# Layer two of batch 4 in seven half-size products, with the squares and sums divided among three engines and all pieces in a new order

## The chip, the cores and the metric

The kernel runs on one core of a Trainium2 chip. The core has a matrix engine (TensorE, PE in the profile; its weight loads are PEld), VectorE (DVE), ScalarE (ACT), GpSimd (POOL) and SyncE (SP). Each has its own queue of instructions that it works through in order; semaphores order one engine behind another. Matrix products go to PSUM, from where VectorE or ScalarE fetch them into SBUF. DMAs are issued from the queues of SP, POOL and ACT. The metric is device time in microseconds. Before the change it is 224.83 us (median of three runs, 224.76 to 225.58).

## The reference

Batches B = 8, heads H = 8, tokens S = 512, states Ns = 32, D = 64, so a token of all heads has H*D = 512 elements. Attention goes both ways between the tokens x and the states, and the result passes through two layers with a squared relu between them:

```python
scores  = scale * np.matmul(x, state.transpose(0, 1, 3, 2))      # softmax over the states
xread   = np.matmul(a, state)
scores2 = scale * np.matmul(state, x.transpose(0, 1, 3, 2))      # softmax over the tokens
sread   = np.matmul(a2, x)
x = concatenate([xread, sread], axis=2).transpose(0, 2, 1, 3).reshape(B * (S + Ns), H * D)
h = x @ w_in                       # 512 -> 2048
r = np.maximum(h, 0.0)
g = s * (r * r) + b
return (g @ w_out).astype(np.float32)   # 2048 -> 512
```

## The kernel before

Layers and attention are worked batch by batch on 512 token rows; the 8 x 32 state rows ("sr") are gathered from all batches and pass through the layers at the end. The attention's second product is folded into the first layer: M = state times w_in is made per batch, so that layer one is the softmax weights A times M.

**Pieces.** Everything is cut into pieces, and the list ORDER names them one after the other. Each piece emits its instructions at once, so ORDER fixes the order in every engine's queue; nothing else schedules. A name holds the piece, the batch, its part, and at the end often the engine (A ScalarE, V VectorE, G GpSimd). Those of the prediction's steps:

- `x.b`, `xn.b`, `win.j`, `wout.q`: loads of x in two layouts, and of quarters of w_in and w_out, from GpSimd's queue. `castx`, `casts`: casts of batch 0's x and first states, which come as FP32 on SP's and ACT's queues.
- Attention of batch b: `xT` (transpose), `T` (scores, TensorE), `U` (transpose back), `mu` (maximum over the states), `D` (difference), `E1` (exponential), `z` (sum and reciprocal), `At` (times reciprocal), `A` (transpose). Batch 0 has these in halves. `keep` copies the scores from PSUM to SBUF. The other direction: `nm`, `nms`, `E2`, `a2`, `aps`, `a2T`, `V`, `srd`.
- `M.b.j` (TensorE) and `Mc.b.j` (copy out of PSUM): a quarter of M. T, M, aps, V and `turn` (transposing the states) use two PSUM tiles of two banks each; the next user of a tile waits for the reader of the last.
- `l.b.f`: one of 16 blocks of layer one, two matmuls of 512 columns on TensorE and a relu on ScalarE into a buffer r of four blocks (`lh`, half the tokens, for batch 0's first blocks, with buffers rh). `s.b.f.n.E`: the square of n blocks from f on, on engine E, into g (`sh` for the halves). `lsr`, `ssr`: the same for the state rows.
- `L.b.rr.q`: four of the 16 matmuls (512 columns) that make 128 rows of the output; four rr by four q make a batch. `out.b.rr` scales, adds the bias and stores. `cps`, `c`, `bias` make the bias from w_out.
- `idle.n`: n matmuls that compute nothing.

**Seven products.** For batches 5, 6, 7 and the state rows layer two isn't done in L pieces. The 512 x 2048 by 2048 x 512 product is taken as 2 x 2 blocks, and seven products of half size take the place of eight: `P.b.u` is one half (8 matmuls of 256 columns) of product u // 2; the half u % 2 takes the even or odd blocks up to, or from, block 8. They need sums of blocks of g (`S.b.1` to `S.b.4`, in halves, S1, S2 and S4 in place, S3 in a tile of its own) and of w_out (`wsum.T1` to `T4`). Products X, W and Y stand in PSUM; `ev.b.X1`, `Y`, `X2`, `W1`, `X3`, `W2`, `X4` add them up in the output tiles osx0 and osx1 on VectorE, and `put` stores. X is added to in PSUM between its evictions, so the next X product waits for the eviction. S2 overwrites what the first product reads, and S4 what the second reads, so they wait for these. The state rows have `S_sr`, `P_sr`, `ev_sr` alike.

In the code, `act_sum` (lines 555 to 564), `weight_sum` (522 to 535) and `sum_sr` (613 to 622) take half h of four of eight block pairs:

```python
A = lambda i, j: block(b, i, j)[:, 4 * h : 4 * h + 4]
```

The buffers r (three) and rh (four) are taken from the pool `rpool` under one tag each, in `layer1` (449 to 456) and `layer1_half` (473 to 482); the squares are `squared` (458 to 462).

Of the kernel before, what the change touches and what calls it, by code (L numbers as in the profile page):

```python
# [11 lines left out]
FP16 = mybir.dt.float16  # L12
# [66 lines left out]
def kernel(  # L79
# [14 lines left out]
    ALU = mybir.AluOpType  # L94
# [6 lines left out]
    P = 128  # L101
# [346 lines left out]

    def layer1(tag, f, terms, ntok):
        hps = ps_h.tile([P, ntok], FP32, name=f"hps_{tag}_{f}", tag="ph")  # L450
        for i, (lhsT, rhs) in enumerate(terms):
            nc.tensor.matmul(hps, lhsT, rhs, start=(i == 0), stop=(i == len(terms) - 1))  # L452
        q, i = f // 4, f % 4
        if (tag, q) not in R_t:
            R_t[tag, q] = rpool.tile([P, 4, ntok], FP16, name=f"r_{tag}_{q}", tag="r")
        nc.scalar.activation(R_t[tag, q][:, i], hps, AF.Relu)  # L456
# [16 lines left out]
    def layer1_half(b, f, p):  # L473
# [7 lines left out]
        r = R_t[b, f, p] = rpool.tile([P, 2, HALF], FP16, name=f"rh_{b}_{f}_{p}", tag="rh", bufs=4)  # L481
# [37 lines left out]

    fast_w = {}  # L520

    def weight_sum(name, h, e):
# [3 lines left out]
        w = w_out16[:, 8 * h : 8 * h + 8]  # L526
        B = [[w[:, k::2, HALF * n : HALF * n + HALF] for n in range(2)] for k in range(2)]
        T = {k: t[:, 4 * h : 4 * h + 4] for k, t in fast_w.items()}
# [26 lines left out]
    def act_sum(b, name, h, e):  # L555

        A = lambda i, j: block(b, i, j)[:, 4 * h : 4 * h + 4]
        out, x, y, op = {
            1: lambda: (A(1, 0), A(1, 0), A(1, 1), ALU.add),
            2: lambda: (A(0, 0), A(1, 0), A(0, 0), ALU.subtract),  # L560
            3: lambda: (fast(b, "S3")[:, 4 * h : 4 * h + 4], A(0, 0), A(1, 0), ALU.subtract),
            4: lambda: (A(0, 1), A(0, 1), A(0, 0), ALU.subtract),
        }[name]()
        e.tensor_tensor(out, x, y, op)  # L564
# [182 lines left out]
```

## Time and profile before

| | |
|---|---|
| median of three runs | 224.83 us |
| the profiled execution | 224.36 us, of which the span is 222.2 us |
| TensorE busy | 210.7 us, 95% of the span |
| VectorE, ScalarE, GpSimd busy | 183.6, 141.8, 43.4 us |
| granted TensorE clock | 1.0 |
| chain that ended last | TensorE 88%, DMA 4%, VectorE 3%, ScalarE 3% |

The span is from the first to the last recorded event; the profiled execution's time has 2.16 us around it. In the rows of groups of instructions the columns are line, engine, operation, what it writes and reads, shapes and count, then busy time in us, mean ns of one, and the idle time just before with its releaser. Rows of the timeline and of the chain begin with the start and the length in us. A matmul's mean (380 ns) holds its way through the array; rows of the chain give the spacing of successive ones. Rows of stretches give, after the length, busy time and count of PE, PEld, DVE, ACT and POOL, then the granted clock, the DMA share and GB/s. In the 40 slices a digit is the busy share in tenths of 5.55 us.

### The profile page before, as it was taken

The numbers are of one execution on the slowest core, as the hardware profiler recorded it, in microseconds if no ns is written. First come the engines' busy times: TensorE is split into PE (matmuls) and PEld (weight loads), VectorE is DVE, ScalarE is ACT, GpSimd is POOL, SyncE is SP. The second block draws the span as 40 slices with busy tenths as digits, with TensorE's granted clock in tenths as the row PEclk, the third lists the DMA queues.
The fourth block names the chain that finished last, engine by engine and source line by source line (L and its number), as shares of the span: only waits on it lengthen the run. The fifth ranks groups of instructions, "written<-read, shape, count | busy, mean of one in ns | idle before, by whom it ended". The sixth has DMA issues, their size and how long they took to land.

```text
span 222.2 us, 4473 instructions
## 1 busy us (share of the span) xinstructions
PE 210.7 (95%) x1816; PEld 115.8 (52%) x1816; DVE 183.6 (83%) x267; ACT 141.8 (64%) x243; POOL 43.4 (20%) x73
## 2 busy tenths in 40 slices
PE   6469999999999999999999999999999999999992
PEld 2234334444444443444454544457766778888881
DVE  1597998889769997989796799889999997966772
ACT  2475895776488869855787479485877858533400
POOL 8245504000273400046002160005200000000000
PEclk9999999999999999999999999999999999999999
DMA  6999993420557892048927397226903500440066
GB/s 158 227 207 206 205 193 58 101 72 20 100 112 117 112 174 50 16 100 120 192 47 133 96 128 124 49 45 101 141 2 65 127 0 3 94 99 0 3 134 149
DMA packets 23416, 22.67 MB, mean 102 GB/s; under 512 B 4196, under 2 KB 16996, under 8 KB 23396
## 3 DMA queue, kind: packets, MB, share of 16 engines
q0 software_dynamic: 16560, 12.26, 38.6%
q1 hardware_dynamic: 6160, 9.97, 18.2%
q8 instruction: 14, 0.23, 0.4%
q10 hardware_dynamic: 676, 0.16, 0.3%
q14 instruction: 6, 0.05, 0.1%
HBM read 25.72 MB, written 8.91 MB: 156 GB/s over the span
## 4 chain that ended last, share of the span: by engine, by line
PE 88%; DMA 4%; DVE 3%; ACT 3%; SPq 1%; issue 0%
PE ops L496 31%; PE hps L452 24%; PE opf_X L137 9%; PE opf_W L137 5%; PE mps L137 4%; DMA xf<-in_x_dram 4%; PE hps_sr L452 3%; PE opf_Y L137 2%; PE vps L137 2%; PE T_None L137 2%; PE aps L137 2%; PE ops_sr_X L137 2%; ACT M L152 1%; DVE xT L289 1%; PE ops_sr_W L137 1%; ACT rh L482 1%
## 5 line engine op out<-in xcount | busy, mean ns | idle before, releaser
L456 ACT ACTIVATE r<-hps 128x512 f16<-128x512 f32 x120 | 69.3, 610 | 29.8 <-PE hps L452 28.4
L496 PE MATMUL ops<-w_out,g 128*128 128x512 f16 x320 | 78.1, 379 | 1.3 <-DVE g L462 1.3
L452 PE MATMUL hps<-A,M 128*128 128x512 f16 x240 | 65.3, 380 | 0.5 <-DVE M L152 0.3
L496 PEld LDWEIGHTS <-g 128*128 128x128 f16 x320 | 30.3, 98 | 38.4 <-issue 2.8
L462 DVE TENSOR_TENSOR g<-r 128x1024 f16<-128x1024 f16 (+1 forms) x39 | 34.5, 897 | 8.1 <-ACT r L456 8.0
L452 PEld LDWEIGHTS <-M 128*128 128x128 f16 x240 | 21.9, 98 | 25.8 <-issue 4.7
L137 PEld LDWEIGHTS <-g 128*128 128x128 f16 x288 | 28.0, 98 | 6.4 <-issue 0.2
L152 ACT CAST M<-mps 128x1024 f16<-128x1024 f32 x28 | 28.0, 1013 | 1.8 <-PE mps L137 1.8
L192 POOL DMA_DIRECT2D xn<-in_x_dram x32 | 18.5, 588 | 29.2 <-PE vps L137 28.3
L506 DVE SCALAR_TENSOR_TENSOR osb<-ops,sb_bc,bias_bc 128x512 f32<-128x512 f32 x20 | 14.7, 734 | 1.0 <-PE ops L496 1.0
L180 POOL COPY ahead<-xT 1x2 f16<-1x2 f16 x5 | 1.8, 367 | 67.0 <-DVE xT L289 67.0
L456 ACT ACTIVATE r_sr<-hps_sr 128x256 f16<-128x256 f32 x16 | 6.2, 385 | 12.8 <-PE hps_sr L452 12.4
L564 DVE TENSOR_TENSOR g<-g 128x1024 f16<-128x1024 f16 x18 | 12.2, 685 | 2.0 <-PE opf_Y L137 1.9
L289 DVE STREAM_TRANSPOSE xT<-xh 128x1024 f32<-128x1024 f32 (+2 forms) x12 | 10.3, 871 | 3.2 <-ACT xh L152 3.2
L333 DVE TENSOR_REDUCE z<-E 128x32 f32<-128x1024 f16 (+1 forms) x9 | 9.9, 1095 | 3.7 <-ACT E L328 3.7
L137 PE MATMUL opf_X<-w_T,g 128*128 128x256 f16 x96 | 11.9, 273 | 0.0
L137 PE MATMUL mps<-w_in,stT 64*32 64x512 f16 x256 | 11.2, 383 | 0.2 <-ACT M L152 0.2
L318 DVE TENSOR_REDUCE mu<-U 128x32 f32<-128x1024 f32 (+1 forms) x9 | 9.9, 1097 | 0.2
L376 ACT ACTIVATE E<-T_None,nms 128x512 f16<-128x512 f32 x8 | 5.5, 691 | 6.9 <-DVE nms L372 4.4
L328 ACT ACTIVATE E<-Dm 128x1024 f16<-128x1024 f32 (+1 forms) x9 | 8.7, 963 | 1.8 <-DVE Dm L322 1.5
L322 DVE TENSOR_TENSOR Dm<-U,mu 128x1024 f32<-128x1024 f32 (+1 forms) x8 | 9.6, 1201 | 0.2
L314 DVE STREAM_TRANSPOSE U<-T_None 128x1024 f32<-128x1024 f32 x7 | 8.7, 1247 | 1.2 <-PE T_None L137 0.8
(94 smaller groups left out, 259.4 us busy)
## 6 DMA issues: line engine op xcount, KB each, us to landing
out_dram<-osb SPq DMA_DIRECT2D x32, 128.0 KB, 2.7
xn<-in_x_dram POOLq DMA_DIRECT2D x32, 128.0 KB, 5.7
xh<-in_x_dram POOLq DMA_DIRECT2D x14, 256.0 KB, 5.2
out_dram<-osx SPq DMA_DIRECT2D x24, 128.0 KB, 2.4
w_in<-in_moe_w_in_dram POOLq DMA_DIRECT2D x8, 256.0 KB, 10.6
w_out<-in_moe_w_out_dram POOLq DMA_DIRECT2D x4, 512.0 KB, 12.7
xf<-in_x_dram SPq DMA_DIRECT2D x4, 256.0 KB, 7.5
out_dram<-osb SPq DMA_DIRECT2D x4, 256.0 KB
```

What stands on the lines that cost most here:

```text
L137: return nc.tensor.matmul(out, lhsT, rhs, start=start, stop=stop, tile_position=tp, is_transpose=is_transpose, skip_group_check=skip,)
L152: (engine.copy if engine is nc.scalar else engine.tensor_copy)(out, in_)
L192: nc.gpsimd.dma_start(out=xn_t[b][32 * jh : 32 * jh + 32].rearrange("t h c d -> t h (c d)"), in_=x[b].rearrange("h (t jh c) d -> jh t h (c ...
L289: nc.vector.transpose(part(out, p, g), part(in_, p, g))
L318: nc.vector.tensor_reduce(part(mu, p), blk(part(at[b]["U"], p)), AX.X, ALU.max)
L333: nc.vector.tensor_reduce(part(z, p), blk(part(at[b]["E1"], p)), AX.X, ALU.add)
L452: nc.tensor.matmul(hps, lhsT, rhs, start=(i == 0), stop=(i == len(terms) - 1))
L456: nc.scalar.activation(R_t[tag, q][:, i], hps, AF.Relu)
L462: e.tensor_mul(g, r, r)
L496: nc.tensor.matmul(ops_t[tag, rr], G_t[tag][:, f, P * rr : P * rr + P], w_out_f(f), start=(f == 0), stop=(f == NKF - 1),)
L506: nc.vector.scalar_tensor_tensor(osb, ops_t.pop((tag, rr)), s_bc, bias_bc, ALU.mult, ALU.add)
L564: e.tensor_tensor(out, x, y, op)
```

## The change

- Batch 4's layer two goes from 16 L and 4 `out` pieces to 14 P, 7 evictions and 4 puts, with its sums S; the sums of w_out are made earlier accordingly.
- Squares, sums, casts of M, D and At are spread differently over ScalarE, VectorE and GpSimd. GpSimd, which had four half squares and one D, gets 9 squares, 5 half squares, 7 sums S, 4 sums of the state rows, 2 weight sums, 2 At and 3 D.
- A sum can be taken whole: `HALVES` has a third entry, h = 2, for all eight block pairs.
- r and rh are taken under one tag per buffer, in turn.
- The idle matmuls are 2, 5 and 9, all ahead of the first scores; they were 11, 6 and 4, the six and the four further on.
- All pieces stand in a new order, the loads too: after w_in's first two quarters it was wout.0, x.1, win.2, wout.1, win.3; it is x.1, win.2, wout.0, win.3, wout.1.

```diff
-    "win.0 win.1 wout.0 x.1 win.2 wout.1 win.3 wout.2 wout.3 idle.11 castx.1.0.V castx.0.0.A xT.0.0.0 "
+    "win.0 castx.0.0.V castx.1.0.A idle.2 idle.5 idle.9 casts.V xT.0.0.0 pair.0.4 xT.0.1.0 T.0.1.0 U.0.0 "
+    "sb mu.0.0 win.1 castx.1.1.A xT.0.1.1 x.1 D.0.V.0 E1.0.0 castx.0.1.V xT.0.0.1 turn.0.4.A z.0.0 "
+    "At.0.V.0 A.0.0 M.0.0.0 Mc.0.0.A keep.0.0 win.2 T.0.0.1 U.0.1 M.0.1.1 Mc.0.1.A mu.0.1 D.0.V.1 "
+    "keep.0.1 E1.0.1 xT.1.0 lh.0.2.0 M.1.0.0 Mc.1.0.A lh.0.0.0 xT.1.1 T.1.1 lh.0.6.0 wout.0 z.0.1 "
+    "At.0.V.1 A.0.1 lh.0.2.1 win.3 U.1 M.0.2.0 lh.0.0.1 Mc.0.2.V wout.1 sh.0.2.1.V keep.1 sh.0.0.0.G mu.1 "
+    "sh.0.2.0.G lh.0.4.0 wout.2 sh.0.4.0.G D.1.V L.0.0.0 l.0.11 M.1.1.0 Mc.1.1.A L.0.1.0 l.0.8 sh.0.6.0.V "
+    "l.0.9 M.0.3.0 Mc.0.3.V M.1.2.1 x.2 l.0.10 Mc.1.2.V wout.3 E1.1 z.1 lh.0.6.1 At.1.V s.0.8.2.A L.0.0.1 "
+    "l.0.13 L.0.1.1 l.0.14 cps.0 cps.1 cps.2 M.1.3.1 A.1 Mc.1.3.V l.0.12 s.0.12.2.V s.0.10.2.G l.0.15 "
+    "s.0.14.2.A L.0.1.2 l.1.4 l.1.7 L.0.0.2 l.1.1 l.1.2 sh.0.6.1.V st xT.2 x.3 pair.4.16 cps.3 L.0.0.3 "
+    "L.0.1.3 c bias lh.0.4.1 l.1.5 T.2.1 l.1.3 out.0.0 out.0.1 U.2 sh.0.0.1.G L.0.3.0 s.1.4.2.A l.1.6 "
...
+    "l.6.0 l.6.1 M.6.3.0 S.5.1.2.V Mc.6.3.A xn.7 xn.1 M.7.0.1 Mc.7.0.A l.6.7 ev.5.Y P.5.6 P.5.7 z.7 "
+    "S.5.2.2.V M.7.1.1 Mc.7.1.A E2.7.1 l.6.15 s.6.0.4.V l.6.14 nm.1 S.5.4.1.G P.5.4 P.5.5 ev.5.X2 ev.5.W1 "
+    "l.6.10 M.7.2.1 S.5.4.0.V E2.7.0 M.7.3.0 Mc.7.3.A At.7.V P.5.8 l.6.13 l.6.4 P.5.9 a2.7 l.6.11 "
...
+    "lsr.0 ssr.0.2.V P.7.8 P.7.9 ssr.2.2.V S_sr.3.0.V ev.7.X3 lsr.9 S.7.4.1.V lsr.8 P.7.10 P.7.11 "
+    "ssr.8.2.A ssr.10.2.V S_sr.3.1.G put.5.1.1 put.6.0.0 S_sr.1.2.V S_sr.2.2.G S_sr.4.0.G put.6.0.1 "
+    "put.6.1.0 put.6.1.1 ev.7.W2 P.7.12 put.7.0.0 put.7.0.1 P.7.13 ev.7.X4 P_sr.0 put.7.1.0 "
+    "ev_sr.0.0.X.0.0 P_sr.1 ev_sr.0.0.Y.1.1 P_sr.2 P_sr.3 put.7.1.1 S_sr.4.1.G ev_sr.0.1.X.0.0 P_sr.4 "
...
+    turns = {}
+
+    def in_turn(shape, name, tag, n):
+        k = turns[tag] = turns.get(tag, -1) + 1
+        return rpool.tile(shape, FP16, name=name, tag=f"{tag}{k % n}", bufs=1)
...
-            R_t[tag, q] = rpool.tile([P, 4, ntok], FP16, name=f"r_{tag}_{q}", tag="r")
+            R_t[tag, q] = in_turn([P, 4, ntok], f"r_{tag}_{q}", "r", 3)
...
+    HALVES = (slice(0, 4), slice(4, 8), slice(0, 8))
...
-        A = lambda i, j: block(b, i, j)[:, 4 * h : 4 * h + 4]
+        sl = HALVES[h]
+        A = lambda i, j: block(b, i, j)[:, sl]
```

More of the change, by code (lines that the diff above doesn't have):

```diff
@@ L480, in layer1_half @@
                 mm(hps[:, i, :], lhsT, part(A, p, g)[:, 0, :], start=(g == 0), stop=(g == NG - 1))
-        r = R_t[b, f, p] = rpool.tile([P, 2, HALF], FP16, name=f"rh_{b}_{f}_{p}", tag="rh", bufs=4)
+        r = R_t[b, f, p] = in_turn([P, 2, HALF], f"rh_{b}_{f}_{p}", "rh", 4)
         nc.scalar.activation(r, hps, AF.Relu)
@@ L525, in weight_sum @@
             fast_w[name] = konst.tile([P, NKF // 2, HALF], FP16, name=f"w_{name}", tag=f"w_{name}")
-        w = w_out16[:, 8 * h : 8 * h + 8]
-        B = [[w[:, k::2, HALF * n : HALF * n + HALF] for n in range(2)] for k in range(2)]
-        T = {k: t[:, 4 * h : 4 * h + 4] for k, t in fast_w.items()}
+        w = w_out16
+        B = [[w[:, k::2, HALF * n : HALF * n + HALF][:, HALVES[h]] for n in range(2)] for k in range(2)]
+        T = {k: t[:, HALVES[h]] for k, t in fast_w.items()}
         a, b = {
@@ L560, in act_sum @@
             2: lambda: (A(0, 0), A(1, 0), A(0, 0), ALU.subtract),
-            3: lambda: (fast(b, "S3")[:, 4 * h : 4 * h + 4], A(0, 0), A(1, 0), ALU.subtract),
+            3: lambda: (fast(b, "S3")[:, sl], A(0, 0), A(1, 0), ALU.subtract),
             4: lambda: (A(0, 1), A(0, 1), A(0, 0), ALU.subtract),
@@ L620, in sum_sr @@
         }[name]
-        out, x, y = (t[:, 4 * h : 4 * h + 4] for t in (S_sr(name), x, y))
+        out, x, y = (t[:, HALVES[h]] for t in (S_sr(name), x, y))
         e.tensor_tensor(out, x, y, op)
```

99 rows, old and new, of the table ORDER are left out of this document.

## The prediction

> **What bounds the kernel now.** I read the page's parts 1, 2 and 4 first, then TensorE's waits, then the timeline of the first 41 us.
>
> ```profile
> PE 210.7 (95%) x1816; PEld 115.8 (52%) x1816; DVE 183.6 (83%) x267; ACT 141.8 (64%) x243; POOL 43.4 (20%) x73
> PE   6469999999999999999999999999999999999992
> ...
> PE 88%; DMA 4%; DVE 3%; ACT 3%; SPq 1%; issue 0%
> ...
> PE T L137 <- DVE xT L289: 2.1, 1, 2.1
> PE dps L660 <- DVE ones L221: 1.5, 1, 1.5
> PE ops L496 <- DVE g L462: 1.3, 1, 1.3
> ...
> 60.00:84.00 24.00, 24.00 (x186) 10.52 (x185) 21.41 (x28) 19.23 (x34) 8.76 (x12) 1.00 0.75 128
> 156.00:180.00 24.00, 24.00 (x211) 16.46 (x208) 23.09 (x33) 17.23 (x30) 0.84 (x2) 1.00 0.46 74
> ```
>
> TensorE carries the chain (88%) and, from slice 5 to the last, is never idle: both 24 us stretches show it busy for 24.00. Its few waits lie in the first 32 us. So time falls only if TensorE gets less work, if the start gets shorter, or if the end does; it rises if any other engine is late by more than the order leaves it. Between start and end VectorE is the nearest (23.09 of 24).
>
> **The products.** The last batch to use whole layer two loses 16 pieces L (64 matmuls of 512 columns) and gets 14 pieces P (112 of 256).
>
> ```profile
> 103.91 0.86 PE ops L496 x4
> 148.58 0.87 PE opf_X L137 x8
> ```
>
> 64 x 0.216 = 13.8 us go, 112 x 0.109 = 12.2 come: **-1.6 us**, on the path, since nothing else sets TensorE's pace there. Its eight stores of 128 KB on the queue of SP stay eight.
>
> **The other engines.** Squares, sums and evictions move; these are the durations.
>
> ```profile
> L462 DVE TENSOR_TENSOR g<-r 128x2048 f16<-128x2048 f16 x16 | 19.4, 1214 | 2.2 <-ACT r L456 2.1
> L462 DVE TENSOR_TENSOR g<-r 128x1024 f16<-128x1024 f16 x23 | 15.2, 677 | 6.0 <-ACT r L456 6.0
> L506 DVE SCALAR_TENSOR_TENSOR osb<-ops,sb_bc,bias_bc 128x512 f32<-128x512 f32 x20 | 14.7, 734 | 1.0 <-PE ops L496 1.0
> L593 DVE SCALAR_TENSOR_TENSOR osx<-opf_X,sb_bc,bias_bc 128x512 f32<-128x512 f32 x9 | 6.7, 742 | 1.3 <-PE opf_X L137 1.3
> L152 DVE CAST M<-mps 128x1024 f16<-128x1024 f32 x4 | 4.8, 1212 | 0.3 <-PE mps L137 0.2
> L343 DVE TENSOR_TENSOR At<-E,rz 128x1024 f16<-128x1024 f16 x7 | 9.1, 1294 | 0.0
> L460 ACT ACTIVATE g<-r 128x1024 f16<-128x1024 f16 x1 | 1.1, 1078 | 0.0
> L152 ACT CAST M<-mps 128x1024 f16<-128x1024 f32 x28 | 28.0, 1013 | 1.8 <-PE mps L137 1.8
> L462 POOL TENSOR_TENSOR g<-rh 128x512 f16<-128x512 f16 x4 | 4.2, 1060 | 4.5 <-ACT rh L482 4.4
> L322 POOL TENSOR_TENSOR Dm<-U,mu 128x1024 f32<-128x1024 f32 x1 | 1.9, 1907 | 4.5 <-DVE mu L318 4.5
> ```
>
> VectorE: squares of 2048 go from 16 to 7 (-10.9), of 1024 from 23 to 15 (-5.4); evictions by output from 20 to 16 (-2.9), by product from 21 to 28 (+5.2); casts of M from 4 to 9 (+6.1); At from 7 to 5 (-2.6), D from 6 to 4 (-2.5). Sums for S, the weights and the state rows, halves and small pieces: about -6, though a fourth batch is summed. In all 183.6 - 19 = some 165 us. ScalarE: 16 more squares of 1024 (+17.2), five fewer casts of M (-5.1), small pieces +1: 155 us. Both stay under TensorE's 197, so this is costed at nothing; TensorE is the cover, and what it would cost without it is the second rival.
>
> GpSimd gets 21 more pieces of 1024 elements, two of 2048 (a square and a sum) and four of 512. A 1024-element piece of FP16 is not in the trace. Between twice the 512 piece (2.1) and the FP32 piece of that length (1.9) I take 1.9; 2048 by the same step is 3.6. 21 x 1.9 + 2 x 3.6 + 4 x 1.06 = 51 us more, 95 in all, behind which its DMA issues of x and xn queue. By the order these have ten and more us of products ahead of the first use.
>
> One fresh tile tag per buffer keeps the number of buffers (three for r, four for rh). It costs nothing unless a slow GpSimd square holds a buffer: the longest, 3.6 us, is in batch 7, and the next user of that buffer is the state rows' layer.
>
> **What two engines at once cost.**
>
> ```profile
> 24.16 1.04 POOL L462 TENSOR_TENSOR g<-rh 128x512 f16<-128x512 f16 x1 [2.24 <-ACT rh L482]
> 24.17 2.11 DVE L322 TENSOR_TENSOR Dm<-U,mu 128x1024 f32<-128x1024 f32 x1
> 131.22 1.22 DVE L322 TENSOR_TENSOR Dm<-U,mu 128x1024 f32<-128x1024 f32 x1
> 70.36 1.27 DVE L343 TENSOR_TENSOR At<-E,rz 128x1024 f16<-128x1024 f16 x1
> 70.50 1.14 POOL L180 COPY ahead<-xT 1x2 f16<-1x2 f16 x1 [4.02 <-DVE xT L289]
> 97.69 0.17 POOL L180 COPY ahead<-xT 1x2 f16<-1x2 f16 x1 [22.70 <-DVE xT L289]
> ```
>
> VectorE's D took 2.11 us instead of 1.22 because GpSimd's product of 1.04 had begun 0.01 us earlier; the two-element copy of GpSimd took 1.14 instead of 0.17 because At was running. A piece with two SBUF inputs on the one waits for the other's. In the changed kernel such pieces of VectorE sum to some 57 us and GpSimd's to 57, so they meet often. If they fall independently over 215 us, GpSimd is computing 57/215 of the time when one of VectorE's 70 such pieces comes up, and holds it for about half of 2 us: +19, giving 184 us, what VectorE carries now. From the last relu piece to its square's first use the order leaves 3 us of TensorE work or more in every later batch (now 2.2), so I count 0.4 us for places where this shows.
>
> [...]
>
> **The start.** Casts, transposes and the attention chain of batch 0 set it. I follow the new order by hand.
>
> ```profile
> 10.36 0.62 ACT L152 CAST xh<-xf 128x512 f16<-128x512 f32 x1 [1.38 <-DMA xf<-in_x_dram]
> 13.40 0.71 DVE L358 STREAM_TRANSPOSE A<-At 128x512 f16<-128x512 f16 x1
> 18.97 0.71 DVE L358 STREAM_TRANSPOSE A<-At 128x512 f16<-128x512 f16 x1
> L314 DVE STREAM_TRANSPOSE U<-T_None 128x1024 f32<-128x1024 f32 x7 | 8.7, 1247 | 1.2 <-PE T_None L137 0.8
> L318 DVE TENSOR_REDUCE mu<-U 128x32 f32<-128x1024 f32 x7 | 8.5, 1214 | 0.1
> L333 DVE TENSOR_REDUCE z<-E 128x32 f32<-128x1024 f16 x7 | 8.5, 1218 | 3.3 <-ACT E L328 3.3
> L353 DVE STREAM_TRANSPOSE A<-At 128x512 f32<-128x512 f32 x7 | 5.0, 707 | 0.1
> 18.00:20.00 2.00, 2.00 (x20) 0.86 (x18) 1.93 (x4) 1.30 (x2) 1.10 (x1) 1.00 1.24 205
> 40.57 0.64 PE L137 MATMUL T_None<-xT,stE 32*32 32x512 f16 x16
> ...
> w_in<-in_moe_w_in_dram POOLq DMA_DIRECT2D x8, 256.0 KB, 10.6
> w_out<-in_moe_w_out_dram POOLq DMA_DIRECT2D x4, 512.0 KB, 12.7
> ```
>
> Pieces on half the tokens I take at half the rows of the whole ones. The last quarter of x lands at 10.36 either way; VectorE's cast (0.5), xT (0.4), z with its reciprocal (0.9), At and A (0.7 each) give A of the first half at 13.6 (now 14.1). T of the second half waits for PSUM: D ends at 10.3, then on ScalarE E1 (0.7), a copy of turned states (0.4), after M (0.4) its cast (1.01): 13.0. T 0.75, U, mu and D 0.7 each, xT of batch 1 (1.25), z 0.9, At and A 0.7 each bring the second A to 19.45 (now 19.7). Squares of the first two half pieces are GpSimd's, 1.06 each behind a relu that ends at 18.8, so the first L starts at 21.15. w_out's first quarter moved behind x.1 and w_in.2: with batch 0's x (two halves of a megabyte), three quarters of w_in and x.1 seven times 0.52 MB are due by it; at the 205 GB/s of the row from some 2 us on, that is 20, in time by 1 us.
>
> From 21.15 TensorE has five L (4.3), eight l (3.5), four M (1.1), one lh and three bias sums (1.3) before l.1.4: ready at 31.5. l.1.4 needs A of batch 1: on VectorE from 19.45 U, a cast of M, a square, mu, D, a square, two casts, z with its reciprocal, At and A: 1.25 + 1.21 + 0.41 + 1.21 + 1.25 + 0.41 + 2.42 + 1.55 + 1.29 + 0.71 = 11.7, plus 0.5 that D waits for a GpSimd square: 31.65. Five l, three L, an lh and two bias steps (5.7) later, T of batch 2 starts at 37.5, against 40.57 now. But two L and two turns of states (2.1 us) that now lie ahead of it come later. **-1.0 us**, between 0 (A of batch 1 a microsecond later) and -2 (the walk's rounding).
>
> Sixteen idle matmuls instead of 21: no cost of their own, as T waits for xT.
>
> **The end.** Three of the last sums go to GpSimd. From the last relu piece to the third state product TensorE has six pieces of 0.87; in that time pass relu 0.39, ScalarE's square (0.6, between the relu and the 1024-element row), sums of 1.06, 0.68 and 1.9, together 4.6, plus hand-overs of some 0.1. In time by 0.1 us, late by 0.3 if GpSimd takes twice 1.06 and a little: inside the 0.4. After the last product both orders have the same two evictions and stores: 0.
>
> **Sum.** 224.36 (span 222.2 and 2.16 around it) - 1.6 - 1.0 + 0.4 = 222.2 for the profiled execution; the median of the three runs lies 0.47 above that, so **222.6 us**.
>
> **The rivals.**
>
> *The gain drains into small waits.* Some evictions have hardly any slack: between batch 5's P.5.5 and P.5.8 lie one l and two M (0.99 us) for an eviction of 0.74, with a maximum over scores of 1.2 directly ahead of it on VectorE; two more places leave 1.3 and 1.8. Two such pieces a full instruction late cost 2.4: no change, 224.4. For: ScalarE and VectorE then run near 11 of 12 us between batch 4's last l and batch 6's. Against: now VectorE has 23.09 of 24 without a wait of TensorE.
>
> *GpSimd and VectorE serialize: slower.* Its place is the stretch from batch 4's first product to batch 6's last, with 62.5 us of TensorE work by the rows above (42 P, 46 l, and M, T, aps and V), 51.3 us of VectorE pieces and 15.9 of GpSimd's computing. If all of GpSimd's time held VectorE up, VectorE would need 67.2, 4.7 more than TensorE: 222.6 + 4.7, **227.3**. It decides from 11 of the 15.9 on. For: the rows of D and ahead. Against: now, from batch 5's first product to batch 6's last, VectorE has 43.9 beside TensorE's 44.5 and TensorE never waits; and GpSimd's D of batch 3 (1.91) held nobody up.
>
> *TensorE starts cold.* The new order leaves it without work from 8.7 to 11.5 and in gaps until 19.5; now the longest is 2.11.
>
> ```profile
> 2.29 0.15 PEld L660 LDWEIGHTS <-ones 128*128 128x128 f16 x1 [0.28 <-issue]
> 2.72 0.15 PEld L660 LDWEIGHTS <-ones 128*128 128x128 f16 x1 [0.28 <-issue]
> 4.32 0.53 PEld L660 LDWEIGHTS <-ones 128*128 128x128 f16 x3 [0.17 <-issue]
> ```
>
> The first idle matmuls start 0.43 us apart, later ones at half of that. If the gaps bring that pace back, some 3 us of dense work after 19.5 take 1.5 longer less what waits hide: 223.8. [...]
>
> **How the numbers follow.** Forecast 0.52 (its own range 221.0 to 223.6), small waits 0.15, serialized 0.22, cold start 0.11. Faster by over 0.5% (under 223.7; 0.5% is what a measurement of this kernel can tell) is the forecast and half the cold start: 0.57. Within: small waits and the other half: 0.21. Slower: 0.22. The range takes the start's -2 at the low end (220.9) and most of the serialized case (227.5).
>
> **What would show it.** Right: T of batch 2 near 37.5; TensorE without waits from 40 us; 112 opf matmuls more; VectorE near 184 busy, D and At of VectorE longer beside GpSimd. Wrong: waits of TensorE on g, S or osx between batches 4 and 7; GpSimd pieces of 1024 above 2.5 us; T of batch 2 after 39; loads of weights 0.2 us apart or more after 19.5.

## The result and the profile after

The changed kernel takes 222.34 us (median of six runs, 221.41 to 223.37) against 224.96 (224.27 to 225.58) for the kernel before, measured side by side: a ratio of 0.9889, 95% interval 0.9857 to 0.9921, or 2.5 us less. The profiled execution took 222.87 us with a span of 221.1.

First the page of the changed kernel: busy times, the slices of TensorE and of its granted clock, the shares of the chain.

```profile
PE 209.8 (95%) x1859; PEld 120.5 (54%) x1859; DVE 172.6 (78%) x235; ACT 152.8 (69%) x258; POOL 99.9 (45%) x100
...
PE   7359999999999999999999999999999999999993
...
PEclk9955999999999999999999999999999999999999
...
PE 87%; DMA 4%; DVE 4%; ACT 1%; SPq 1%; issue 1%; DVEq 0%
```

TensorE is still the bound and full from slice 5 to the last. VectorE lost 11 us, ScalarE gained 11, GpSimd 56.5. The clock differs too: half speed in slices 3 and 4 (from 11.1 to 21.3 us), where the profiled execution of before had 1.0 throughout. Not every execution of before has that: of the 89 timed beside the experiments' kernels, 48 had a mean granted clock of 0.996 or more and took 224.48 us on average, the other 41 (0.980 to 0.992) 225.27. The changed kernel's six have 0.977 to 0.985.

The waits of TensorE (in total, times, longest), and then two stretches of the middle:

```profile
PE mps L136 <- ACT stT L151: 3.3, 1, 3.3
...
PE T L136 <- ACT M L151: 1.1, 1, 1.1
PE mps L136 <- ACT Ts L309: 0.7, 1, 0.7
...
PE opf_X L136 <- DVE g L571: 0.2, 1, 0.2
```

```profile
132.00:156.00 24.00, 24.00 (x279) 16.63 (x276) 23.49 (x30) 19.56 (x33) 17.01 (x19) 1.00 0.64 99
...
180.00:212.00 32.00, 31.77 (x328) 26.61 (x327) 19.69 (x29) 14.79 (x30) 15.19 (x8) 1.00 0.18 38
```

Only one wait, 0.2 us, lies behind the start, although VectorE is busy for 23.49 of 24 us between 132 and 156 and GpSimd for 17.01 beside it.

Two places of the timeline cut the span into three comparable parts: T of batch 2 (38.73 in the changed kernel) and the first state product (211.05). The rows also show the gap ahead of the first M and the first L:

```profile
11.65 0.63 PE L136 MATMUL mps<-w_in,stT 64*32 64x512 f16 x8 [3.28 <-ACT stT L151]
...
22.28 1.03 PE L501 MATMUL ops<-w_out,g 128*128 128x512 f16 x4
...
38.73 0.64 PE L136 MATMUL T_None<-xT,stE 32*32 32x512 f16 x16
...
211.05 1.04 PE L136 MATMUL ops_sr_X<-w_out,g_sr 128*128 128x256 f16 x8
```

The same marks of every kernel profiled, from the same rows of its timeline (the middle is the first state product less T of batch 2; the last column is how long half clock lasted in the first 34 us, from the granted clock of stretches of 1 us):

| kernel | T of batch 2 | middle | ratio to before, 95% interval | half clock, us |
|---|---|---|---|---|
| before | 40.57 | 171.29 | 1 | 0.0 |
| changed | 38.73 | 172.32 | 0.9889 [0.9857, 0.9921] | 10.2 |
| l4 | 38.15 | 174.48 | 0.9987 [0.9963, 1.0012] | 6.8 |
| one_tag | 41.02 | 172.33 | 0.9984 [0.9957, 1.0011] | 10.2 |
| before_turns | 41.67 | 171.49 | 1.0003 [0.9976, 1.0030] | 3.4 |
| before_fewer_idle | 41.88 | 171.30 | 1.0028 [1.0007, 1.0050] | 10.2 |
| warm | 39.14 | 172.33 | 0.9888 [0.9866, 0.9910] | 0.0 |
| loads | 40.52 | 172.29 | 0.9973 [0.9948, 0.9999] | 13.6 |
| warm_loads | 40.71 | 172.32 | 0.9976 [0.9947, 1.0006] | 10.2 |
| gp_early | 40.67 | 173.25 | 1.0053 [1.0023, 1.0083] | 10.2 |
| gp_S | 38.70 | 174.29 | 1.0003 [0.9974, 1.0032] | 10.2 |
| gp_att | 38.85 | 174.15 | 1.0002 [0.9968, 1.0037] | 10.2 |
| gp_to_v | 42.25 | 179.43 | 1.0378 [1.0335, 1.0421] | 10.2 |
| ev_later | 38.15 | 171.93 | 0.9891 [0.9857, 0.9925] | 6.8 |

A difference of two ratios is turned into microseconds with 224.9 us; with such intervals it is uncertain by some 0.9 us.

### The profile page after: what moved, and what is told of

Same layout as the page of the kernel before. It is cut to its first block, busy times and chain, and to the rows that moved or that the text cites. A ratio compares the mean times of both kernels' runs of the same rounds, so it can differ in the third digit from the quotient of the medians.

```text
span 221.1 us, 4579 instructions
## 1 busy us (share of the span) xinstructions
PE 209.8 (95%) x1859; PEld 120.5 (54%) x1859; DVE 172.6 (78%) x235; ACT 152.8 (69%) x258; POOL 99.9 (45%) x100
## 4 chain that ended last, share of the span: by engine, by line
PE 87%; DMA 4%; DVE 4%; ACT 1%; SPq 1%; issue 1%; DVEq 0%
PE ops L501 25%; PE hps L457 24%; PE opf_X L136 12%; PE opf_W L136 6%; PE mps L136 4%; DMA xf<-in_x_dram 3%; PE opf_Y L136 2%; PE vps L136 2%; PE aps L136 2%; PE ops_sr_X L136 2%; PE hps_sr L457 2%; PE T_None L136 2%; PE hph L136 1%; DMA out_dram<-osx 1%; PE ops_sr_W L136 1%; SPq L608 1%
## 5 line engine op out<-in xcount | busy, mean ns | idle before, releaser
L501 PE MATMUL ops<-w_out,g 128*128 128x512 f16 x256 | 62.1, 379 | 0.0
L467 POOL TENSOR_TENSOR g<-r 128x1024 f16<-128x1024 f16 (+1 forms) x9 | 18.8, 2101 | 14.9 <-ACT r L461 14.9
L467 DVE TENSOR_TENSOR g<-r 128x1024 f16<-128x1024 f16 (+1 forms) x22 | 20.5, 945 | 2.7 <-ACT r L461 2.6
L571 POOL TENSOR_TENSOR g<-g 128x1024 f16<-128x1024 f16 (+1 forms) x5 | 13.6, 2731 | 18.6 <-DVE g L571 18.6
L465 ACT ACTIVATE g<-r 128x1024 f16<-128x1024 f16 (+1 forms) x19 | 21.6, 1148 | 0.2
L321 POOL TENSOR_TENSOR Dm<-U,mu 128x1024 f32<-128x1024 f32 x3 | 7.0, 2343 | 20.4 <-DVE mu L317 20.3
L600 DVE SCALAR_TENSOR_TENSOR osx<-opf_X,sb_bc,bias_bc 128x512 f32<-128x512 f32 x12 | 8.9, 741 | 7.1 <-PE opf_X L136 6.3
L571 DVE TENSOR_TENSOR g<-g 128x1024 f16<-128x1024 f16 (+1 forms) x15 | 13.3, 915 | 1.2 <-POOL S L571 1.1
L629 POOL TENSOR_TENSOR g_sr<-g_sr 128x512 f16<-128x512 f16 (+1 forms) x4 | 6.0, 1521 | 12.6 <-ACT g_sr L465 12.5
L151 DVE CAST M<-mps 128x1024 f16<-128x1024 f32 x9 | 10.8, 1208 | 0.8 <-PE mps L136 0.8
```

Of the source, the lines that this page charges most:

```text
L151: (engine.copy if engine is nc.scalar else engine.tensor_copy)(out, in_)
L465: nc.scalar.activation(g, r, AF.Square)
L467: e.tensor_mul(g, r, r)
L501: nc.tensor.matmul(ops_t[tag, rr], G_t[tag][:, f, P * rr : P * rr + P], w_out_f(f), start=(f == 0), stop=(f == NKF - 1),)
L600: nc.vector.scalar_tensor_tensor(out, fast(b, name[0]), s_bc, out if plus else bias, ALU.mult, ALU.add)
```

## The experiments

**l4: the products.**

```diff
-P.4.0 ... P.4.13, ev.4.*, put.4.*, S.4.*
+L.4.0.0 ... L.4.3.3, out.4.0 ... out.4.3
```

> The changed kernel with batch 4's layer two in whole pieces again (16 L and 4 evictions in the places of 14 P and 7 evictions, without its sums S); all else in the same order. Theory 'TensorE's work': 1.6 us more, 223.9. Rival 'the order alone made the gain, the products bring waits': within 0.4 us of the changed kernel's 222.3 or below, since VectorE has 8 us and GpSimd 4 us less to do.

Ratio 0.9987: without the products 0.0098, or 2.2 us, of the gain is gone, and order, spread and tags alone give nothing that can be told from no change. The trace has it in the middle (174.48 against 172.32, 2.16 us). 1.6 of it is the work; in l4 one wait is longer besides:

```profile
201.27 1.05 PE L136 MATMUL opf_X<-w_T,g 128*128 128x256 f16 x8 [0.80 <-DVE g L571]
```

It is the wait of 0.23 us of the changed kernel, at the same product of batch 7, and accounts for the other 0.6; why it is longer there, no run shows.

**one_tag: the tags of r and rh.**

```diff
-in_turn([P, 4, ntok], f"r_{tag}_{q}", "r", 3)
+rpool.tile([P, 4, ntok], FP16, name=f"r_{tag}_{q}", tag="r")
-in_turn([P, 2, HALF], f"rh_{b}_{f}_{p}", "rh", 4)
+rpool.tile([P, 2, HALF], FP16, name=f"rh_{b}_{f}_{p}", tag="rh", bufs=4)
```

> The changed kernel with the buffers r (three) and rh (four) taken again under one tag each, as before the change. If the tags only name the buffers, nothing: T of batch 2 and the first state product within 0.3 us, 222.3. If a release under one tag waits for the slowest of the readers (the GpSimd squares of 1.9 us), relu pieces start later and the time is 1 us or more longer.

0.9984: 0.0095 or 2.1 us slower, and T of batch 2 2.29 us later with an identical middle. The prediction had this edit at nothing. The timeline of ScalarE with one tag, then with the tags in turn:

```profile
23.05 0.60 ACT L487 ACTIVATE rh<-hph 128x512 f16<-128x512 f32 x1 [1.65 <-DVE g L467]
...
25.77 0.60 ACT L487 ACTIVATE rh<-hph 128x512 f16<-128x512 f32 x1 [1.22 <-DVE g L467]
```

```profile
22.13 0.60 ACT L487 ACTIVATE rh<-hph 128x512 f16<-128x512 f32 x1 [0.58 <-PE hph L136]
...
23.51 0.61 ACT L487 ACTIVATE rh<-hph 128x512 f16<-128x512 f32 x1
```

These are the half relu pieces lh.0.0.1 and lh.0.4.0, the fifth and sixth to ask for one of four buffers. With one tag they wait for VectorE's squares, which stand on its queue behind a cast, a maximum and a D:

```profile
22.54 0.41 DVE L467 TENSOR_TENSOR g<-rh 128x512 f16<-128x512 f16 x1
22.87 1.21 DVE L317 TENSOR_REDUCE mu<-U 128x32 f32<-128x1024 f32 x1
24.12 1.23 DVE L321 TENSOR_TENSOR Dm<-U,mu 128x1024 f32<-128x1024 f32 x1
25.26 0.42 DVE L467 TENSOR_TENSOR g<-rh 128x512 f16<-128x512 f16 x1
```

The second relu starts 2.26 us later than with tags in turn, which is the whole delay of T of batch 2. In the built program the queues of all engines hold the same instructions in the same order; what differs is what some relu pieces wait for:

```
one tag:  rh_0_1 [VectorE, TensorE]    rh_4_0 [VectorE, TensorE]
in turn:  rh_0_1 [TensorE, ScalarE, GpSimd]    rh_4_0 [TensorE, ScalarE]
```

With tags in turn the fifth tile takes the first tile's buffer, whose square is GpSimd's and done at 20.97. With one tag it is given that of lh.0.2.1, and the sixth that of lh.0.6.0, whose squares are VectorE's. Both the tags and an order that hands pieces out of turn to two engines belong to that.

**before_turns: the tags alone.** The same edit the other way round, in the kernel before.

> The kernel before, with nothing changed but the buffers r and rh, which are taken under one tag each in turn as in the changed kernel. Taken back from the changed kernel, these tags cost 2.3 us ahead of T of batch 2, since two half relu pieces then wait for VectorE's squares. If the tags help only because the new order has its squares out of the order of its relu pieces, they do nothing here: 224.8, T of batch 2 within 0.3 us of 40.57. If they free the relu pieces in general, 1 us or more is gained: 223.8 or less.

224.74 against 224.62 us, ratio 1.0003: nothing. (The profiled execution has T of batch 2 at 41.67, outside the 0.3 us; TensorE waited there 2.8 us instead of 2.1 for the xT of batch 0's second half, and its clock fell for 3.4 us. The middle, 171.49 against 171.29, is the same.) So the tags are worth 2.1 us in the new order and nothing in the old.

**warm: the cold clock.** Twelve more idle matmuls close the gap from 8.37 to 11.65.

```diff
-turn.0.4.A z.0.0
+turn.0.4.A idle.12 z.0.0
```

> The changed kernel with twelve more idle matmuls behind the turn of the first states, in the 3.3 us in which TensorE has nothing to do (8.4 to 11.7). Theory 'cold start': the half clock from 11.5 to 21.8 us cost what the start is late against the walk, so the granted clock stays 1.0, the first L starts at 21.2 instead of 22.28, T of batch 2 at 37.5 instead of 38.73, and the time falls by 1.2 us to about 221.1. Rival 'VectorE's chain sets the start': the clock is full but T of batch 2 stays at 38.5 or later, time 222.0 to 222.5.

The clock stays at 1.0 in the profiled execution and two others (0.985 to 0.992 in the remaining three), and the time does not move (0.9888). The timelines of TensorE and VectorE in the profiled execution say why:

```profile
22.00 1.02 PE L501 MATMUL ops<-w_out,g 128*128 128x512 f16 x4 [0.36 <-DMA w_out<-in_moe_w_out_dram]
...
36.70 0.58 DVE L252 STREAM_TRANSPOSE stE<-stn 128x384 f32<-128x384 f32 x1 [1.46 <-DMA stn<-in_state_dram]
```

The first L waits for w_out, which lands at 22.0, and the pairing of the states for a DMA. But that load is not equally late in every execution. In warm it was issued at 10.02; in the changed kernel's trace at 8.95, and with the 12.0 us that it took it lay ready at about 21.0. There the first L, at 22.28, came straight behind TensorE's own pieces. So did it in ev_later (below), whose start is the same and whose second A ends at the same time (19.87 against 19.82), but whose clock was back at 19.6 instead of 21.3. The changed kernel, then ev_later:

```profile
8.95 0.75 POOL L205 DMA_DIRECT2D w_out<-in_moe_w_out_dram  x1 [2.70 <-DMA w_in<-in_moe_w_in_dram]
...
21.39 1.05 PE L136 MATMUL hph<-A,M 128*128 128x256 f16 x8
```

```profile
20.82 1.05 PE L136 MATMUL hph<-A,M 128*128 128x256 f16 x8
21.70 1.03 PE L501 MATMUL ops<-w_out,g 128*128 128x512 f16 x4
...
38.15 0.64 PE L136 MATMUL T_None<-xT,stE 32*32 32x512 f16 x16
```

The longer half clock goes with 0.58 us at the first L and the same 0.58 us at T of batch 2: cold clock and landings lie so close together that taking away the one leaves the other.

**loads and warm_loads: the two landings.** w_out's first quarter and the states are issued earlier, once with the cold clock and once with the idle matmuls.

```diff
-x.1 D.0.V.0 ... lh.0.6.0 wout.0 ... sh.0.4.0.G D.1.V ... sh.0.6.1.V st xT.2
+x.1 wout.0 D.0.V.0 ... lh.0.6.0 ... sh.0.4.0.G st D.1.V ... sh.0.6.1.V xT.2
```

> The changed kernel with two loads issued earlier on GpSimd's queue: w_out's first quarter right behind x.1 (ahead of w_in's third quarter), and the states of the other batches ahead of x.2 instead of after w_out's last quarter. TensorE keeps its cold clock. If only the landings of these loads set the start, both being masked by the slow clock here, nothing moves: first L at 22.3, T of batch 2 at 38.7, time 222.3 (within 0.3). Rival, the slow TensorE work is waiting for w_out already: first L near 21.3 and T of batch 2 near 37.8, 221.4. Third possibility, w_in's third and fourth quarter come late and M waits for them: T of batch 2 after 39.2, 222.9 or more.

> The same two loads earlier, and the 12 idle matmuls that keep TensorE at full clock. With both, nothing of the two known causes is left: if the cold clock and the landings hid each other, the first L starts near 21.2, the wait of the pairing of states (1.46 us on the DMA of the states) is gone, T of batch 2 comes at 37.5 to 38.0 and the time is 221.2 (221.0 to 221.5). Rival, the chain of attention on VectorE sets T of batch 2 anyway: T of batch 2 stays at 38.5 or later, and the time at 222.3.

0.9973 and 0.9976: both some 2 us slower than the changed kernel. The third possibility holds. With loads, TensorE and VectorE:

```profile
20.98 0.62 PE L136 MATMUL mps<-w_in,stT 64*32 64x512 f16 x7 [0.38 <-DMA w_in<-in_moe_w_in_dram]
...
21.66 1.23 DVE L151 CAST M<-mps 128x1024 f16<-128x1024 f32 x1 [1.69 <-PE mps L136]
```

TensorE now waits for a quarter of w_in, and VectorE stands for 1.69 us ahead of the cast of that M. In every 2 us from 8 to 26 of the changed kernel the DMA moves 204 to 219 GB/s (the stretches' last column):

```profile
10.00:12.00 2.00, 0.35 (x8) 0.12 (x8) 1.97 (x5) 0.89 (x2) 0.61 (x1) 0.77 1.23 206
...
18.00:20.00 2.00, 1.89 (x21) 0.56 (x6) 1.90 (x5) 1.02 (x3) 1.09 (x2) 0.50 1.24 206
...
24.00:26.00 2.00, 2.00 (x24) 0.84 (x24) 1.97 (x2) 2.00 (x4) 1.78 (x3) 1.00 1.24 206
```

So the loads follow one another without a gap; here one that went earlier made another one late.

**before_fewer_idle: the idle matmuls of the old order.**

```diff
-idle.6 ... idle.4
```

> The kernel before without idle.6 and idle.4, which leaves TensorE without work from about 8.0 to 11.5 us. Theory 'cold start': the clock goes to half there as in the changed kernel, and the time rises by 0.5 to 1.5 us (225.5 to 226.4). Rival: these ten matmuls did nothing for the clock, which stays at 1.0, and the time stays within 0.3 us of 224.9.

1.0028, 0.6 us slower, and the clock fell in all twelve executions (0.973 to 0.983): the cold start holds for the old order, at the low end of its range. The old order needs its idle matmuls a little; the new one gains nothing by more (warm).

**gp_to_v, gp_early, gp_S, gp_att: what GpSimd's pieces carry.** All 27 whole pieces go back to VectorE at their places in the order; then three of their groups one at a time.

```diff
-s.0.10.2.G s.1.0.2.G s.1.2.2.G s.2.8.2.G s.2.10.2.G
+s.0.10.2.V s.1.0.2.V s.1.2.2.V s.2.8.2.V s.2.10.2.V
```

> The changed kernel with all GpSimd squares of 1024 and 2048, sums, At and D given back to VectorE, in the same order (the five half squares stay). VectorE's busy time goes from 172.6 to some 189 us (22 more, 6 of holds less). Theory 'the three engines are needed': in the stretches where VectorE has 23 of 24 us already TensorE now waits for g and S, 2 to 5 us more (224.5 to 227). Rival 'VectorE had room, as in the kernel before with 184 us': within 0.5 us of 222.3.

> The changed kernel with five squares of batches 0 to 2 (1024 elements each, s.0.10, s.1.0, s.1.2, s.2.8, s.2.10) on VectorE instead of GpSimd; all other pieces of GpSimd stay. When all 27 pieces went back the time rose by 11 us, of which 3.5 lay ahead of T of batch 2. If those 3.5 come from the early squares on VectorE's queue, T of batch 2 comes at 41 to 42.3 and the time is 224.5 to 226. If the pieces cost only through VectorE's total load, five pieces of 0.68 are 3.4 us of 173 busy and nothing is late: 222.3.

> The changed kernel with GpSimd's seven half sums S of batches 4 to 7 on VectorE, everything else as it is. With all 27 pieces back the time rose by 11 us, 3.4 of them through the five early squares alone. If VectorE's order around the products is what has no slack, these seven sums (0.68 us each on VectorE, 4.8 in all, in stretches where it is busy for 23.5 of 24 us) cost 2 to 4 us, nearly all between T of batch 6 and the first state product: 224.3 to 226.3. If the shared access of the two engines costs as much as GpSimd's work saves, then nothing: within 0.7 of 222.3.

> The changed kernel with GpSimd's three D, two At and the two halves of the third weight sum on VectorE. VectorE gets 3 x 1.23 + 2 x 1.30 + 2 x 0.68 = 7.7 us, spread over batches 3 to 7. If VectorE's lateness there is worked off before TensorE needs it (the scores are needed long after), 222.3 to 222.8. If every piece in front of an eviction or a sum counts, 3 to 5 us more, 225.3 to 227.3, with TensorE's waits on VectorE's g or osx between batches 4 and 7.

The whole costs 0.0489, 11.0 us; the five early squares 3.7, the seven half sums S 2.6, the three D, two At and two halves of a weight sum 2.5. All at once cost far more than the 2 to 5 us expected. gp_S came out as its first theory had it and gp_early near it (its trace has 1.9 us ahead of T of batch 2 and 0.9 in the middle); gp_att lies between its two. What is left of the 11 (2.2) belongs to the later squares and the sums of the state rows, or to what the groups do together; these were not run alone. VectorE's load does not explain it: with all back it is 186.8 us busy, 80% of the span, hardly more than the 183.6 of the kernel before, and in none of the stretches of 24 us from 36 to 180 does it have more than 22.65, where the changed kernel has 23.49 without a wait. What the traces show instead is the place in the queue. In gp_early (TensorE):

```profile
34.30 0.60 PE L501 MATMUL ops<-w_out,g 128*128 128x512 f16 x2 [2.38 <-DVE g L467]
```

It is L.0.0.2, which needs s.0.10; that square now stands on VectorE behind two casts of M, z, At, A, a third cast and another square, where GpSimd did it at 27.72. In gp_S and then gp_att (TensorE's timeline):

```profile
193.35 1.05 PE L136 MATMUL opf_W<-w_out,g 128*128 128x256 f16 x8 [1.17 <-DVE g L571]
```

```profile
97.49 1.02 PE L501 MATMUL ops<-w_out,g 128*128 128x512 f16 x4 [0.35 <-DVE osb L511]
115.91 1.02 PE L501 MATMUL ops<-w_out,g 128*128 128x512 f16 x4 [0.27 <-DVE osb L511]
131.84 0.59 PE L457 MATMUL hps<-A,M 128*128 128x512 f16 x2 [0.38 <-ACT r L461]
```

A product of batch 6 waits for a sum; in gp_att two evictions and a relu come late by a few tenths. Of gp_att's 1.83 us more in the middle these waits show 1.0; the rest is in gaps that the waits do not list.

**ev_later: the one wait in the middle.**

```diff
-ssr.12.2.A ev.7.X1 S.7.2.1.V ... S.7.2.0.V ev.7.Y P.7.4
+ssr.12.2.A S.7.2.1.V ... S.7.2.0.V ev.7.X1 ev.7.Y P.7.4
```

> The changed kernel with the first eviction of batch 7 (ev.7.X1) moved behind the last half sum S2 of batch 7 on VectorE's queue; it waits for the stores of batch 6's osx0, and the sums no longer wait with it. If the 0.23 us wait of TensorE near 199.7 comes from that chain, it goes: 0.2 us less, 222.1. If the product waits for the eviction itself as long as before, 222.3; if the eviction now comes late for the next X product, up to 0.5 us more, 222.8.

The changed kernel there:

```profile
194.27 2.12 POOL L571 TENSOR_TENSOR g<-g 128x1024 f16<-128x1024 f16 x1
194.35 2.59 DVE L571 TENSOR_TENSOR g<-g 128x1024 f16<-128x1024 f16 x1 [1.09 <-POOL S L571]
...
197.68 0.75 DVE L600 SCALAR_TENSOR_TENSOR osx<-opf_X,sb_bc,bias_bc 128x512 f32<-128x512 f32 x1 [0.74 <-DMA out_dram<-osx]
...
199.69 1.05 PE L136 MATMUL opf_X<-w_T,g 128*128 128x256 f16 x8 [0.23 <-DVE g L571]
```

osx0 has one buffer, and batch 6's stores of it land at 197.56; the eviction waits for them, the half sums S.7.2 stand behind it, and P.7.4 behind these. With the eviction moved, the wait is gone and the middle is 0.39 us shorter (0.23 of it the wait), but the times are the same (222.34; 0.9891): 0.2 to 0.4 us is less than six runs can tell.

## Why the prediction was right, and where its steps were not

The forecast was 222.6, and 222.34 was measured. The likeliest case came out, but not by all of its steps.

*The products, -1.6 us.* Right: l4 shows 2.2 in the time and 2.16 in the trace, of which 1.6 is TensorE's work and 0.6 a wait that is shorter beside the products.

*The start, -1.0 us.* The path was right up to the second A (19.82 against 19.45), and again from the first L to T of batch 2 (16.45 us against 16.35). In between, the first L came at 22.28 instead of 21.15, so T of batch 2 came at 38.73 instead of 37.5; less the 2.1 us of work that comes later, that is +0.3. The step that failed is the one that let GpSimd's squares release the first L. They were done on time (20.97), and w_out's first quarter, due at 20, was there at about 21.0; last were TensorE's own pieces between the second A and the first L. Of the 1.1 us, 0.4 are the later A and 0.6 the half clock (ev_later). Part of the rest of the miss is the one execution taken as the start of before, which had full clock: other traces of the old order (before_fewer_idle, before_turns) have T of batch 2 at 41.88 and 41.67, and of the new start (l4, ev_later, gp_S, gp_att) at 38.15 to 38.85. From the means, 41.37 and 38.52, the start gives -2.85 + 2.1 = -0.7, though one of the three old ones lacks idle matmuls.

*One tag per buffer, 0 us.* Wrong, and the largest single miss: 2.1 us. Read as a change by itself it does nothing, as before_turns shows; but the walk through the start took for granted that no relu piece waits for a buffer, and that holds only with these tags. The forecast was right because the tags were there, not because they were costed.

*Squares, sums and attention on three engines, at nothing under TensorE.* The result agrees, for only the wait of 0.2 us is left on them. GpSimd's durations were close: 1.91 for a square of 1024 (predicted 1.9), 3.6 for 2048, 1.04 for 512; a sum takes 2.12, and some pieces stood behind VectorE's, which brings the means of the sums in place, D and At to 2.40, 2.34 and 2.32: 99.9 us busy and not 95. What the step called cover, TensorE's 197 us, isn't what matters: gp_to_v has nearly the VectorE load of before and is 11 us slower than the changed kernel.

*Two engines at once, 184 us busy on VectorE.* Wrong in size. Groups of VectorE and one of GpSimd in the changed kernel:

```profile
L467 POOL TENSOR_TENSOR g<-r 128x1024 f16<-128x1024 f16 x8 | 15.2, 1914 | 14.9 <-ACT r L461 14.9
...
L571 POOL TENSOR_TENSOR g<-g 128x1024 f16<-128x1024 f16 x4 | 9.6, 2398 | 10.0 <-DVE g L571 10.0
```

```profile
L467 DVE TENSOR_TENSOR g<-r 128x1024 f16<-128x1024 f16 x15 | 12.1, 820 | 1.8 <-ACT r L461 1.6
L571 DVE TENSOR_TENSOR g<-g 128x1024 f16<-128x1024 f16 x12 | 9.7, 844 | 1.2 <-POOL S L571 1.1
L342 DVE TENSOR_TENSOR At<-E,rz 128x1024 f16<-128x1024 f16 x5 | 7.4, 1475 | 0.1
L321 DVE TENSOR_TENSOR Dm<-U,mu 128x1024 f32<-128x1024 f32 x4 | 5.7, 1422 | 0.1
```

Against 677 and 1294 ns (the rows of before), 1.22 us (D alone) and 0.69 (the median of these sums), the four groups are held up by 15 x 0.14 + 12 x 0.16 + 5 x 0.18 + 4 x 0.20 = 5.7 us, where the estimate was 19. The two engines do not meet at random: the trace has six places where a piece of these groups is held, and the estimate's 57/215 of 70 pieces would make 19. For most of GpSimd's pieces the order has VectorE at evictions, casts and transposes. Where they meet, it costs in full: the sum at 194.35 took 2.59 us instead of 0.68 beside GpSimd's piece of 2.12. In each of the six VectorE's piece took longer by what was left of GpSimd's, less some 0.13 us: 0.21 us longer at 187.61, 1.91 at 194.35. Casts of M, which read PSUM, and sums z, which read one tile of SBUF, were not held: the five and three that began beside a piece of GpSimd took 1.21 us each (medians), those alone 1.19 and 1.21. GpSimd is held in turn, which the estimate left out: three of its pieces of 1024 took 2.70, 2.82 and 2.94 us, above the 2.5 that the prediction named as a sign of being wrong, each begun within 0.25 us behind a piece of VectorE. TensorE waited for none of them.

*0.4 us for places.* About right: TensorE's middle grew from 2.3 to 2.8 us beyond its work (171.29 less 169.0; 172.32 less 169.54, estimates from counts of matmuls by their spacing).

*The end, 0.* From the first state product to the end it is 10.05 us, against 10.34: -0.3. The sums of the state rows came in time.

*The sum.* In the two profiled spans: +0.3 - 1.6 + 0.5 - 0.3 = -1.1 (222.2 to 221.1). A further 0.35 lies outside the spans, whose surroundings take 1.77 instead of 2.1 us in every kernel with the new order; no view shows why, and this stays open. Profiled, that is 1.5 less (224.36 to 222.87). The medians differ by 2.6, because before's profiled execution, at full clock, was 0.6 below its median and the changed kernel's, one of the two with the longest half clock, 0.5 above. That the forecast lies within 0.3 us of the median is therefore in part luck: the profiled spans fall by 1.1 us where 2.2 were forecast, and the difference is made up by the 0.35 outside them and by which executions were profiled.

*The rivals.* Small waits: one of 0.2 us where 2.4 were feared; the place named first (between P.5.5 and P.5.8) was in time. Serializing: no; GpSimd and VectorE were busy for 17.01 and 23.49 of 24 us without a wait of TensorE. Taking the work back from GpSimd is what makes it slower. Cold start: it happened as described (half clock from 11.1 to 21.3), and cost the profiled execution 0.6 us by the comparison with ev_later, where the prediction had a loss of 1.2; warm's median shows nothing of it, as the loads land no earlier. The estimate had some 3 us of it; the slow pace at the start of before's trace lasted 2.86 us (1.46 to 4.32), the half clock 10.2.

## What to carry to other kernels

An order worked out by hand and the way its buffers are handed out are one change: walk through who frees each buffer, not only how many there are. An engine's busy share tells little about what a piece moved onto it will cost; look at what stands ahead of it on the queue when its reader needs it. When loads follow one another without a gap, moving one forward may only move the lateness (loads was 1.9 us slower than the changed kernel), and a cold clock beside them may cost little (warm: 0.9888 against 0.9889). A profile is one execution: look at the clocks and times of the others before taking it as the start of a sum.

## What the runs showed of the hardware

TensorE's granted clock fell to half in or behind gaps of 2.6 to 3.28 us, and once without such a gap. In the changed kernel it fell at 11.1 us, 2.7 us into a gap of 3.28; in l4 and ev_later 2.0 and 0.8 us behind the end of a gap of 2.6. In warm_loads there was no such gap, yet the clock fell in a stretch of scattered work:

```profile
13.00:14.00 1.00, 0.93 (x18) 0.45 (x11) 0.97 (x3) 0.17 (x2) 0.30 (x2) 1.00 1.12 208
14.00:15.00 1.00, 0.47 (x4) 0.27 (x3) 0.97 (x2) 1.00 (x2) 0.48 (x1) 0.81 1.16 200
15.00:16.00 1.00, 0.49 (x8) 0.12 (x7) 0.96 (x3) 0.55 (x2) 0.00 (x0) 0.50 1.24 208
```

The longest waits around it are 1.12 and 1.03 us. The profiled execution of warm had as little work in the same stretch (0.93 us of the 2 from 14 on, where warm_loads has 0.97) and stayed at 1.0. And the clock came back late: the changed kernel's TensorE, busy for 1.57 to 2.00 of every 2 us from 14 on, had half clock until 21.3. Where it fell, half clock lasted 3.4, 6.8, 10.2 or 13.6 us (the table's last column), one to four steps of 3.4.

In none of these four traces was TensorE without work for longer than 3.28 us before the clock fell. What sets the steps, and why as little work brought half clock in warm_loads and not in warm, no run shows.

For 1024 elements GpSimd took 1.9 us for a square, 1.94 for an At (at 109.55 us of the changed kernel) and 1.91 for a D (at 148.96), and 2.12 for a sum, in place (at 194.27) or into another tile. None of these had begun behind a piece of VectorE with two SBUF inputs; longer ones had: the At of 2.70 at 80.86 (VectorE's square from 80.63), the D of 2.82 at 122.89 (from 122.73), the sum of 2.94 at 158.88 (from 158.63).
